# Loading and turning the first batch's queries in two parts, with moved loads, in a talking-heads attention and feed-forward kernel

## The chip, the cores and the metric

The kernel runs on one core of a Trainium2 chip. The metric is the device time of one execution in microseconds (us). The core has a matrix engine (TensorE, PE in the profile; its weight loads are PEld), VectorE (DVE), ScalarE (ACT), GpSimd (POOL) and SyncE (SP), which run their own instruction streams and wait for one another by semaphores, and sixteen DMA engines, which take work from queues. POOL issues the loads that change the type (float32 in memory, bf16 on the chip), SP the copies inside the core.

## The reference

For eight batches of twelve heads, 448 positions and 64 dimensions, with `w_pre` and `w_post` 12 by 12:

```python
scores = scale * np.matmul(q, k.transpose(0, 1, 3, 2))
scores = np.einsum('bhij,hg->bgij', scores, w_pre)
attn = softmax(scores)                       # over the last axis
attn = np.einsum('bhij,hg->bgij', attn, w_post)
x = np.matmul(attn, v)                       # heads side by side: 3584 x 768
h = np.maximum(x @ w_in, 0.0)                # w_in 768 x 2048
out = h * h @ w_out                          # w_out 2048 x 768
```

## The kernel before

**Steps.** A batch has 45 steps (`NT`) of ten queries each (`IQ`), so there are 360 steps, and one loop over `i` (line 578) writes out the order of TensorE and POOL by hand for all of them (`tc.manual_schedule`, line 524). The other engines' orders follow the program order and `tc.issue_after`. In step `i`, `mix` (line 456) makes the mixed scores of ten queries for all twelve heads at once, 120 rows, and ScalarE takes the exponential (line 471): the n-th exponential in the trace marks step n. POOL then scales `post` by the reciprocal sums (`pn`, line 481), and four steps later (`LAG`) `unmix` (line 487) multiplies the exponentials by it on TensorE; VectorE copies the result out of PSUM (line 502). After fifteen steps `av_unit` multiplies by the values, and when a batch is done `ffn1_unit` and `ffn2_unit` run as filler between the steps. PSUM has eight banks for all of this.

**Two ways to the mixed scores.** From step 20 on (`FUSED`), a *score burst* (line 394) multiplies 128 queries by all keys for a few heads at a time, ScalarE and VectorE copy the scores to a tile `S` (lines 416 and 418; two buffers), and SP's DMAs gather ten queries with all heads into a tile `G` (line 435; twelve buffers), on which line 467 does the mixing. A burst writes into a buffer that earlier gathers must have finished reading. `BURSTS` says at which gathers the bursts of the next block are made. In the first twenty steps there is no time for that: `mix_queries` (line 218) multiplies the turned queries by the mixing weights on VectorE, and `fused_part` (line 445) multiplies the keys by them, six matmuls per step.

**The front.** Queries and keys of the first batch come in twelve loads from POOL's queue (line 103), each of two heads on one half of the partitions: for `u` = 0, 1, 2 two of queries, then two of keys. Each row holds seven positions, since a partition holds seven consecutive positions (`RQ`), and `turn_unit` (line 227) transposes a unit of queries or keys with 28 small matmuls (line 239) and copies it out (line 241). While loads are on their way TensorE multiplies a zeroed tile (`still`, line 93). `mix_queries(u, 0, NEAR)` makes steps 0 to 3, `NEAR` to `SOON` steps 4 to 11, and `SOON` to `FUSED` steps 12 to 19. `make_identity` writes the matrix for the transposes with two POOL instructions.

**Later loads.** `KQ_AT`, `KQ_LATER`, `V1_AT`, `V_LATER`, `W1_AT`, `W2_AT` give the steps at which POOL issues the loads of queries and keys, values and weights of the next batches; the staging tiles of queries and of keys have one buffer each. `TURN` says at which step of a batch the next batch's keys (first three numbers) and queries are turned; the turn needs both halves of the load. The squares of the feed-forward's first half (line 320) are made by POOL, or by VectorE for columns from 300 on; `EARLY` starts those of the first batch by thirds of the columns, at steps 21, 29, 38 and 52.

Of the kernel before, what the change touches and what calls it, by code (L numbers as in the profile page):

```python
# [14 lines left out]
B, H, S, D = 8, 12, 448, 64  # L15
DMODEL = H * D
DFF = 2048
NPAIR = H // 2
FT = DFF // 128
R = 4  # L20
RQ = 7
PQ = S // RQ
HQ = H // 2
IQ = 10
# [2 lines left out]
FUSED = 20  # L27
SOON = 12
FQ = FUSED * IQ
NEAR = 4  # L30
# [2 lines left out]
BURSTS = {0: ([4, 8], [5, 8])}  # L33
for _b in range(1, B):
    STARTS[_b], FIRST[_b], BURSTS[_b] = (0, 128, 256, 384), (0, 13, 26, 39), ([5, 8], [5, 8], [6], [2, 4])
BURSTS[1] = ([5, 8], [7, 10], [6], [2, 4])
BURSTS[2] = ([7, 10], [5, 8], [6], [2, 4])
GATHERS_AT = 8
FIRST_AT = (3, 5, 7)
HALF = H // 2  # L40
TT = 15
TQ = TT * IQ
LAG = 4
AHEAD = 10
SCALE = 1.0 / 8.0
TURN = {0: (20, 22, 23, 24, 26, 27), 1: (24, 24, 24, 28, 28, 28), B: (2 + LAG,) * 3 + (17 + LAG,) * 3}
KQ_LATER = {1: (26, 28, 37, 41), B: (22, 25, 28, 31)}
V_LATER = {1: (30, 32, 34), B: (34, 37, 40)}
KQ_AT = {1: (4, 7, 10, 12), 2: (49, 51, 53, 55)}
W1_AT = (-1, 1, 3, 14, 16, 18)  # L50
W2_AT = (27, 29, 31, 33, 36, 39, 42, 45)
V1_AT = (46, 48, 24)
EARLY = ((21, 0, 0, 2), (29, 0, 2, 4), (38, 1, 0, 4), (52, 2, 0, 4))
FFN2_AT = 60
STILL = (10, 2, 2, 2, 1)
SOONEST = 3
MAIN = 3 * 128

# [2 lines left out]
def kernel(  # L61
# [36 lines left out]
    def stage_tile(name):  # L98
        return stage.tile([P, HQ, RQ, D], BF16, name=name, tag=name, bufs=1)

    def load(t, src, b, a, h0=0, h1=HQ):

        nc.gpsimd.dma_start(out=t[PQ * a:PQ * a + PQ, h0:h1, :, :].rearrange("p h r d -> p h (r d)"),
                            in_=src[b, HQ * a + h0:HQ * a + h1, :, :].rearrange("h (p r) d -> p h (r d)", r=RQ))

    staged = {}
    staged[0] = (stage_tile("qst"), stage_tile("kst"))
    ident = consts.tile([P, P], BF16, name="ident")
    for u in range(NPAIR // 2):
        for w, src in enumerate((q, k)):  # L110
            for x in range(2):
                load(staged[0][w], src, 0, x, 2 * u, 2 * u + 2)
                if u + w == 0 and x == 1:
                    masks.make_identity(nc, ident[:, :])

    def wcol(w, name, eng):
        t = consts.tile([P, H], F32, name=name)
# [106 lines left out]
                                    in1=wrep[:, u + 3 * y, :, :].unsqueeze(1).to_broadcast([P, t1 - t0, H, IQ]),  # L224
                                    op=ALU.mult)

    def turn_unit(b, which, u, eng=None):

        store, name = (qTs, "qT") if which == 0 else (kTs, "kT")
        if b not in store:  # L230
            store[b] = work.tile([P, NPAIR, S], BF16, name=name, tag=name, bufs=2)
        src = staged[b][which]
        got = [bank("tr_ps", BF16) for _ in range(2)]
        for r in range(RQ):
            c = PQ * (r if which == 0 or r == RQ - 1 else 2 * (r % 3) + r // 3)
            for hh in range(2):
                for x in range(2):
                    rs = slice(PQ * x, PQ * x + PQ)
                    nc.tensor.transpose(got[x][64 * hh:64 * hh + 64, c:c + PQ], src[rs, 2 * u + hh, r, :], ident[rs, rs])  # L239
        for x in range(2):  # L240
            (eng or nc.vector.tensor_copy)(out=store[b][:, u + 3 * x, :], in_=got[x][:, 0:S])

    def turn_units(b):
        return [(250, lambda u=u, w=w: turn_unit(b, w, u)) for w in (1, 0) for u in range(NPAIR // 2)]
# [56 lines left out]
    def ffn1_unit(b, ft, k=1, n0=0, n1=S):  # L301

        ps = bank("h_ps")
        n = n1 - n0
        for j in range(k):
            f = ft + j
            for c2 in range(NPAIR):
                nc.tensor.matmul(ps[:, n * j:n * j + n], lhsT=w1[f // 8][:, c2, f % 8 * 128:f % 8 * 128 + 128],  # L308
                                 rhs=xts[b][:, c2, n0:n1], start=(c2 == 0), stop=(c2 == NPAIR - 1))
        if n0 == 0 and ft % 2 == 0:  # L310
            h2ts[(b, ft // 2)] = ffnp.tile([P, 2, MAIN], BF16, name="h2", tag="h2", bufs=FT // 2 + 1)
        h2 = h2ts[(b, ft // 2)][:, ft % 2:ft % 2 + k, :]
        hr = ffnp.tile([P, S], F32, name="hr", tag="hr", bufs=2)
        nc.scalar.activation(out=hr[:, 0:k * n], in_=ps[:, 0:k * n], func=ACT.Relu)  # L314
        hr = hr[:, 0:k * n].rearrange("p (k n) -> p k n", k=k)
        eng = nc.vector if n0 >= 2 * TQ else nc.gpsimd
        last = tails[:, ft:ft + k, 64 * (b % 2):64 * (b % 2) + 64]
        for x, y, o, dst in ((n0, min(n1, MAIN), 0, h2), (max(n0, MAIN), n1, MAIN, last)):
            if x < y:
                eng.tensor_tensor(out=dst[:, :, x - o:y - o], in0=hr[:, :, x - n0:y - n0], in1=hr[:, :, x - n0:y - n0],  # L320
                                  op=ALU.mult)
# [202 lines left out]
    with tc.manual_schedule(engines={PE, POOL}):  # L524
# [1 line left out]
            load_v(0, x)  # L526
        still(STILL[0])
        for u in range(NPAIR // 2):
            turn_unit(0, 0, u)
            mix_queries(u, 0, NEAR)  # L530
            if u == 1:
                with tc.issue_after(mixes[(1, 0)].ins):
                    mix_queries(0, NEAR, SOON)
            if u == 2:
                for t in range(SOONEST):
                    fused_part(t, 0)
            else:
                still(STILL[1 + 2 * u])
            turn_unit(0, 1, u, nc.scalar.copy)
            if u < 2:  # L540
                still(STILL[2 + 2 * u])
        for t in range(SOONEST):
            fused_part(t, 1)
        with tc.issue_after(mixes[(2, 0)].ins):
            mix_queries(1, NEAR, SOON)
            mix_queries(2, NEAR, SOON)
        loads = {}
        ahead = [FUSED]

# [28 lines left out]
        for i in range(-1, end):  # L578
            for f in loads.get(i, []):
                f()  # L580
            if i < 0:
                continue
            if i == NT // 2:
                for (_, n), (t, order) in orders.items():
                    half_pre(n, t, order)
            s0 = steps[i] if i < len(steps) else None
            s1 = steps[i - LAG] if LAG <= i < len(steps) + LAG else None
            if s0:
                b, t = s0
                if t == 0:  # L590
                    if b + 1 < B:
                        for x, u in enumerate(turn_units(b + 1)):
                            at_step(i + TURN.get(b, TURN[B])[x], u)
            early = [x for x in bounds if x > i]
            rest = early[0] - i if early else (1 + LAG - i) % NT + 1
            rest = min(rest, end - i) if i > len(steps) - NT // 2 else rest
            share = sum(w for w, _ in filler) / rest / 2
            now = timed.pop(i, [])
            if s0:
                mix(s0)  # L600
            now_at[0] = i
            send_stores(i)
            for w, f in now:
                f()
                owed[0] -= w if not FFN2_AT <= i < 2 * NT else 0
            fill(share)
            if s1:
                unmix(s1)
                b1, t1 = s1
                if t1 % TT == TT - 1:  # L610
                    for u in av_units(b1, t1 // TT):
                        at_step(i + 3, u)
                if t1 == NT - 1:
                    at_step(i + 3 if b1 else FFN2_AT, (0, lambda b1=b1: filler.extend(ffn_units(b1))))
            if 2 < i < 6:
                with tc.issue_after(mixes[(2, NEAR)].ins):
                    mix_queries(i - 3, SOON, FUSED)
            if i in FIRST_AT:
                x = 2 * FIRST_AT.index(i)
                score_burst(0, 0, [x, x + 1])  # L620
            if i == 3:
                with tc.issue_after(mixes[(2, NEAR)].ins):
                    make_post()
                    make_orders()
                    clear_values()
            for _ in range(2 if i >= GATHERS_AT else 0):
                if ahead[0] > min(max(i + AHEAD, FIRST[0][1] - 1), len(steps) - 1):
                    break
                b2, t2 = steps[ahead[0]]
                gather((b2, t2))  # L630
                ahead[0] += 1
                blk2 = max(x for x in range(len(FIRST[b2])) if FIRST[b2][x] <= t2)
                nxt = blocks.index((b2, blk2)) + 1
                first = BURSTS[b2][blk2]
                if nxt < len(blocks) and t2 - FIRST[b2][blk2] in first:
                    x = first.index(t2 - FIRST[b2][blk2])
                    score_burst(*blocks[nxt], [3 * x, 3 * x + 1, 3 * x + 2])
                    if filler and filler[0][1] in second:
                        w, f = filler.pop(0)
                        f()  # L640
                        owed[0] -= w
            if i + 1 < end:
                fill(share)
# [35 lines left out]
```

## Time and profile before

| | |
|---|---|
| time, median of three runs | 583.04 us (582.56 to 585.91) |
| the profiled execution's own time | 583.95 us |
| its span, first to last instruction | 582.2 us |
| TensorE busy | 567.5 us (97%) |
| VectorE, ScalarE, POOL busy | 398.8, 379.7, 378.9 us |
| moved by DMA | 72.28 MB, mean 124 GB/s |
| chain that ended last | PE 89%, DMA 6%, ACT 2% |

The span is cut into stretches in the views below; the third column pair of a stretch is what each engine was busy. A chain of waits is followed back from the last instruction to whatever released each step. A name such as `L239` is a line of the kernel. The granted TensorE clock is 1.00 over the whole span.

### The profile page before, as it was taken

The numbers are of one execution on the slowest core, as the hardware profiler recorded it, in microseconds if no ns is written. First come the engines' busy times: TensorE is split into PE (matmuls) and PEld (weight loads), VectorE is DVE, ScalarE is ACT, GpSimd is POOL, SyncE is SP. The second block draws the span as 40 slices with busy tenths as digits, with TensorE's granted clock in tenths as the row PEclk, the third lists the DMA queues.
The fourth block names the chain that finished last, engine by engine and source line by source line (L and its number), as shares of the span: only waits on it lengthen the run. The fifth ranks groups of instructions, "written<-read, shape, count | busy, mean of one in ns | idle before, by whom it ended". The sixth has DMA issues, their size and how long they took to land.

```text
span 582.2 us, 18463 instructions
## 1 busy us (share of the span) xinstructions
PE 567.5 (97%) x6750; PEld 362.6 (62%) x6752; DVE 398.8 (69%) x980; ACT 379.7 (65%) x1090; POOL 378.9 (65%) x844
## 2 busy tenths in 40 slices
PE   7999999999999999999999999999999999999996
PEld 3667777556566566566566665666665665666554
DVE  6858868778676777866877668867877668655011
ACT  2768978588876557864877648775777548862410
POOL 6657985655877448774778547785577647774830
PEclk9999999999999999999999999999999999999999
DMA  9999998797568864796558954697544865422113
GB/s 130 159 193 184 187 199 173 152 168 175 111 108 149 145 128 87 126 157 141 101 100 135 176 117 93 120 145 154 107 73 71 137 139 104 84 46 55 29 27 82
DMA packets 84043, 72.28 MB, mean 124 GB/s; under 512 B 18768, under 2 KB 80496, under 8 KB 83952
## 3 DMA queue, kind: packets, MB, share of 16 engines
q0 software_dynamic: 37856, 33.04, 37.1%
q1 hardware_dynamic: 45514, 37.86, 29.5%
q8 instruction: 53, 0.87, 0.6%
q10 hardware_dynamic: 582, 0.21, 0.2%
q14 instruction: 38, 0.31, 0.1%
HBM read 47.28 MB, written 11.01 MB: 100 GB/s over the span
## 4 chain that ended last, share of the span: by engine, by line
PE 89%; DMA 6%; ACT 2%; POOL 1%; issue 1%; DVE 1%; ACTq 0%; POOLq 0%
PE h_ps L308 24%; PE o_ps L353 24%; PE m_ps L467 11%; PE at_ps L496 10%; PE ot_ps L254 5%; DMA G<-S 5%; PE s_ps L406 5%; PE m_ps L453 4%; PE tr_ps L239 2%; PE ot_ps L261 2%; PE at_ps L500 2%; DMA kst<-in_k_dram 1%; PE s_ps L412 1%; ACT e L471 1%; ACT S L416 1%
## 5 line engine op out<-in xcount | busy, mean ns | idle before, releaser
L502 DVE CAST at<-at_ps 128x480 bf16<-128x480 f32 (+1 forms) x360 | 206.6, 592 | 63.1 <-PE at_ps L500 46.0
L471 ACT ACTIVATE e<-m_ps 120x448 bf16<-120x448 f32 x360 | 195.7, 550 | 82.1 <-PE m_ps L467 45.4
L481 POOL TENSOR_SCALAR pn<-post,rc 120x120 bf16<-120x120 bf16 (+1 forms) x340 | 122.4, 370 | 137.6 <-DVE rc L478 76.0
L308 PE MATMUL h_ps<-xt,w 128*128 128x448 bf16 (+2 forms) x960 | 165.8, 315 | 1.0 <-ACT S L416 0.9
L353 PE MATMUL o_ps<-w,h 128*128 128x384 bf16 x768 | 138.8, 326 | 0.1
L467 PE MATMUL m_ps<-G,pre 120*120 120x448 bf16 (+1 forms) x340 | 121.3, 357 | 2.5 <-ACT S L416 1.4
L308 PEld LDWEIGHTS <-w 128*128 128x128 bf16 x960 | 83.4, 98 | 54.1 <-issue 4.9
L496 PE MATMUL at_ps<-pn,e 120*128 120x120 bf16 x1080 | 115.8, 215 | 1.3 <-POOL pn L481 1.1
L496 PEld LDWEIGHTS <-e 120*128 120x128 bf16 x1080 | 85.9, 98 | 45.7 <-issue 3.6
L320 POOL TENSOR_TENSOR h<-hr 128x384 bf16<-128x384 f32 (+1 forms) x128 | 103.1, 806 | 11.1 <-ACT hr L314 9.5
L353 PEld LDWEIGHTS <-h 128*128 128x128 bf16 x768 | 72.4, 98 | 50.5 <-issue 8.0
L314 ACT ACTIVATE hr<-h_ps 128x448 f32<-128x448 f32 (+2 forms) x136 | 72.0, 530 | 47.0 <-PE h_ps L308 39.4
L416 ACT CAST S<-s_ps 128x448 bf16<-128x448 f32 x177 | 82.3, 551 | 11.1 <-PE s_ps L406 7.2
L418 DVE CAST S<-s_ps 128x448 bf16<-128x448 f32 x141 | 80.0, 615 | 3.9 <-DMA G<-S 2.8
L471 ACT ACTIVATION_READ_ACCUMULATOR e<-m_ps 120x1 f32 x360 | 75.5, 210 | 0.0
L362 DVE COPY osb<-o_ps 128x384 f32<-128x384 f32 x54 | 30.0, 556 | 55.4 <-PE o_ps L353 55.3
L478 DVE RECIPROCAL rc<-sm 120x1 f32<-120x1 f32 (+1 forms) x192 | 31.0, 162 | 40.6 <-ACT e L471 28.0
L467 PEld LDWEIGHTS <-pre 120*120 120x120 bf16 (+1 forms) x340 | 45.0, 132 | 17.5 <-issue 8.6
L267 ACT CAST xt<-ot_ps 128x450 bf16<-128x450 f32 (+1 forms) x48 | 25.7, 534 | 26.7 <-PE ot_ps L261 26.3
L484 POOL TENSOR_TENSOR en<-e,rc 120x128 bf16<-120x128 bf16 (+1 forms) x112 | 42.8, 382 | 0.0
L254 PE MATMUL ot_ps<-at,v 128*64 128x150 bf16 x864 | 41.7, 229 | 0.0
L406 PE MATMUL s_ps<-kT,qT 64*128 64x448 bf16 x276 | 39.0, 352 | 0.2
(66 smaller groups left out, 502.7 us busy)
## 6 DMA issues: line engine op xcount, KB each, us to landing
G<-S SPq DMA_DIRECT2D x276, 105.0 KB
out_dram<-osb POOLq DMA_DIRECT2D x48, 192.0 KB, 4.7
kst<-in_k_dram POOLq DMA_DIRECT2D x14, 336.0 KB, 5.9
qst<-in_q_dram POOLq DMA_DIRECT2D x14, 336.0 KB, 5.8
G<-S SPq DMA_DIRECT2D x70, 52.5 KB
v<-in_v_dram POOLq DMA_DIRECT2D x8, 384.0 KB, 9.1
w<-in_moe_w_in_dram POOLq DMA_DIRECT2D x6, 512.0 KB, 8.5
w<-in_moe_w_out_dram POOLq DMA_DIRECT2D x8, 384.0 KB, 9.2
```

The lines of the kernel that those rows point to most:

```text
L254: nc.tensor.matmul(ps[64 * hh:64 * hh + 64, TQ * y:TQ * y + TQ], lhsT=vts[b % 2][:, g, r, :], rhs=at[:, r, g, :, :].rearrange("p t i -> p ...
L308: nc.tensor.matmul(ps[:, n * j:n * j + n], lhsT=w1[f // 8][:, c2, f % 8 * 128:f % 8 * 128 + 128], rhs=xts[b][:, c2, n0:n1], start=(c2 == 0 ...
L314: nc.scalar.activation(out=hr[:, 0:k * n], in_=ps[:, 0:k * n], func=ACT.Relu)
L320: eng.tensor_tensor(out=dst[:, :, x - o:y - o], in0=hr[:, :, x - n0:y - n0], in1=hr[:, :, x - n0:y - n0], op=ALU.mult)
L353: nc.tensor.matmul(ps[:, 0:384], lhsT=lhsT, rhs=w2[ft // 4][:, ft % 4, nt * 384:(nt + 1) * 384], start=(ft == 0), stop=(ft == FT - 1))
L416: nc.scalar.copy(out=sb[:, h, :], in_=ps[:, 0:S])
L418: nc.vector.tensor_copy(out=sb[:, h, :], in_=ps[:, 0:S])
L467: nc.tensor.matmul(ps[0:n, 0:S], lhsT=m[0:n, 0:n], rhs=Gs.pop(s)[0:n, :], start=True, stop=True)
L471: nc.scalar.activation(out=e[0:n, x, :], in_=ps[0:n, 0:S], func=ACT.Exp, scale=SCALE, accum_out=sm[0:n, x:x + 1])
L481: nc.gpsimd.tensor_scalar(out=esb[(b, t - z)][1][0:rows, :], in0=(post_gi if fused else post)[0:rows, :], scalar1=rc[0:rows, z:z + 1], sca ...
L496: nc.tensor.matmul(ps[:, RG * r:RG * r + RG], lhsT=e[0:n, tl % 2, P * r:P * r + P], rhs=pn[0:n, :], start=True, stop=True)
L502: nc.vector.tensor_copy(out=ats[(b, third)][:, 0:k, :, tl, :], in_=ps[:, 0:k * RG].rearrange("p (r g i) -> p r g i", r=k, i=IQ))
```

## The change

The first batch's queries are loaded in two parts: first positions 0 and 1 of each row (`RF = 2`, 128 of the 448 columns) for all heads, two loads in place of six; then the keys; then the other five positions, two loads. The identity is cleared by VectorE, and POOL's other instruction for it stands among the key loads. The first part of the queries is turned and mixed ahead of all keys; the second part is turned in step 3 of the loop. The mixing of steps 4 to 11 is done in two blocks of four steps. One of the six copies of turned keys goes from ScalarE to VectorE. The zeroed tile is multiplied 19 times in place of 17. Score bursts and gathers of the first batch move by one step. Loads of batches one to three, two turns and one pair of bursts get other steps. Four squares of 300 columns (third 1, `ft` 8 to 14) go from POOL to VectorE.

```diff
+RF = 2
-BURSTS[1] = ([5, 8], [7, 10], [6], [2, 4])
+BURSTS[1] = ([5, 8], [7, 10], [6], [3, 5])
-GATHERS_AT = 8
-FIRST_AT = (3, 5, 7)
+GATHERS_AT = 9
+FIRST_AT = (4, 6, 8)
+REST_AT = 3
-TURN = {0: (20, 22, 23, 24, 26, 27), 1: (24, 24, 24, 28, 28, 28), B: (2 + LAG,) * 3 + (17 + LAG,) * 3}
-KQ_LATER = {1: (26, 28, 37, 41), B: (22, 25, 28, 31)}
-V_LATER = {1: (30, 32, 34), B: (34, 37, 40)}
-KQ_AT = {1: (4, 7, 10, 12), 2: (49, 51, 53, 55)}
+TURN = {0: (20, 22, 23, 24, 26, 27), 1: (20, 20, 20, 28, 28, 28), B: (2 + LAG,) * 3 + (17 + LAG,) * 3}
+KQ_LATER = {1: (22, 24, 37, 41), B: (22, 25, 28, 31)}
+V_LATER = {1: (53, 55, 57), B: (34, 37, 40)}
+KQ_AT = {1: (4, 7, 10, 12), 2: (52, 54, 58, 61)}
-V1_AT = (46, 48, 24)
+V1_AT = (46, 49, 24)
-STILL = (10, 2, 2, 2, 1)
+STILL = (13, 3, 3)
...
-    def load(t, src, b, a, h0=0, h1=HQ):
+    def load(t, src, b, a, h0=0, h1=HQ, r0=0, r1=RQ):
...
+    for x in range(2):
+        load(staged[0][0], q, 0, x, r1=RF)
+    nc.vector.memset(ident[:, :], 0.0)
     for u in range(NPAIR // 2):
-        for w, src in enumerate((q, k)):
-            for x in range(2):
-                load(staged[0][w], src, 0, x, 2 * u, 2 * u + 2)
-                if u + w == 0 and x == 1:
-                    masks.make_identity(nc, ident[:, :])
+        for x in range(2):
+            load(staged[0][1], k, 0, x, 2 * u, 2 * u + 2)
+        if u == 1:
+            masks.make_identity(nc, ident[:, :], nomemset=True)
+    for x in range(2):
+        load(staged[0][0], q, 0, x, r0=RF)
...
-    def turn_unit(b, which, u, eng=None):
+    def turn_unit(b, which, u, engs=None, r0=0, r1=RQ):
...
-        for r in range(RQ):
+        for r in range(r0, r1):
...
-            (eng or nc.vector.tensor_copy)(out=store[b][:, u + 3 * x, :], in_=got[x][:, 0:S])
+            copy = engs[x] if engs else nc.vector.tensor_copy
+            copy(out=store[b][:, u + 3 * x, PQ * r0:PQ * r1], in_=got[x][:, PQ * r0:PQ * r1])
...
-        eng = nc.vector if n0 >= 2 * TQ else nc.gpsimd
+        eng = nc.vector if n0 >= 2 * TQ or n0 and ft >= FT // 2 else nc.gpsimd
...
         for u in range(NPAIR // 2):
-            turn_unit(0, 0, u)
+            turn_unit(0, 0, u, r1=RF)
             mix_queries(u, 0, NEAR)
-            if u == 1:
-                with tc.issue_after(mixes[(1, 0)].ins):
-                    mix_queries(0, NEAR, SOON)
+        still(STILL[1])
+        for u in range(NPAIR // 2):
             if u == 2:
+                with tc.issue_after(mixes[(2, 0)].ins):
+                    mix_queries(0, NEAR, 2 * NEAR)
+
+            def between(out, in_):
+                with tc.issue_after(mixes[(0, NEAR)].ins):
+                    mixes["kT"] = nc.vector.tensor_copy(out=out, in_=in_)
+
+            turn_unit(0, 1, u, (nc.scalar.copy, nc.scalar.copy if u < 2 else between))
+            if u == 0:
+                still(STILL[2])
+            else:
                 for t in range(SOONEST):
-                    fused_part(t, 0)
-            else:
-                still(STILL[1 + 2 * u])
-            turn_unit(0, 1, u, nc.scalar.copy)
-            if u < 2:
-                still(STILL[2 + 2 * u])
-        for t in range(SOONEST):
-            fused_part(t, 1)
-        with tc.issue_after(mixes[(2, 0)].ins):
-            mix_queries(1, NEAR, SOON)
-            mix_queries(2, NEAR, SOON)
+                    fused_part(t, u - 1)
+        for t0 in range(NEAR, SOON, NEAR):
+            with tc.issue_after(mixes["kT" if t0 == NEAR else (2, t0 - NEAR)].ins):
+                for u in range(t0 == NEAR, NPAIR // 2):
+                    mix_queries(u, t0, t0 + NEAR)
...
-            if 2 < i < 6:
-                with tc.issue_after(mixes[(2, NEAR)].ins):
-                    mix_queries(i - 3, SOON, FUSED)
+            if i == REST_AT:
+                for u in range(NPAIR // 2):
+                    turn_unit(0, 0, u, r0=RF)
+            if FIRST_AT[0] <= i < FIRST_AT[0] + 3:
+                with tc.issue_after(mixes[(2, SOON - NEAR)].ins):
+                    mix_queries(i - FIRST_AT[0], SOON, FUSED)
...
-                with tc.issue_after(mixes[(2, NEAR)].ins):
+                with tc.issue_after(mixes[(2, SOON - NEAR)].ins):
                     make_post()
```

## The prediction

> **What bounds the kernel now.** I read the page's first part, then TensorE by stretches, the timeline of TensorE and POOL at the front, the chain, and the waits of the two stretches with holes.
>
> ```profile
> PE 567.5 (97%) x6750; PEld 362.6 (62%) x6752; DVE 398.8 (69%) x980; ACT 379.7 (65%) x1090; POOL 378.9 (65%) x844
> ```
>
> TensorE is the bound: of a span of 582.2 us it is idle 14.7. Any saving must come out of those, or out of work on TensorE that no one needs (the zeroed tile). The table of stretches (length, then busy us of PE, PEld, DVE, ACT, POOL) shows where they are:
>
> ```profile
> 0.00:14.74 14.74, 10.64 (x190) 4.98 (x193) 9.04 (x32) 3.21 (x5) 10.13 (x21) 1.00 0.92 131
> 14.74:30.00 15.26, 15.20 (x102) 9.52 (x103) 12.61 (x34) 10.70 (x31) 9.98 (x20) 1.00 1.09 156
> 75.00:90.00 15.00, 12.72 (x200) 10.37 (x198) 9.73 (x24) 10.94 (x34) 14.29 (x29) 1.00 1.18 199
> 105.00:120.00 15.00, 13.04 (x251) 7.99 (x250) 11.90 (x33) 8.38 (x28) 9.09 (x21) 1.00 0.89 163
> 577.72:582.20 4.48, 0.00 (x1) 0.00 (x0) 0.36 (x1) 0.32 (x1) 0.00 (x0) 1.00 0.20 56
> ```
>
> The tail (4.48) is not touched. Idle is 2.28 at 75 to 90 and 1.96 at 105 to 120; 180 to 530 has 0.6 in all. The first 14.74 us look 10.64 busy, but the work in them that counts is 168 transposes at 0.34 us per 28 (2.04) and six matmuls at 0.19 (1.14): 3.2 us. The rest is zeroed tile and waiting for loads. TensorE's timeline shows the last key unit, the chain shows what comes behind it:
>
> ```profile
> 13.50 0.21 PE L239 MATMUL tr_ps<-ident,kst 64*64 64x64 bf16 x1
> 14.33 0.41 PE L239 MATMUL tr_ps<-ident,kst 64*64 64x64 bf16 x27 [0.61 <-DMA kst<-in_k_dram]
> ```
>
> ```profile
> 8.41 5.87 DMA kst<-in_k_dram
> 14.29 0.04 issue
> 14.33 0.41 PE tr_ps L239 x27
> 14.74 3.54 PE m_ps L453 x18
> ```
>
> The twelfth load, issued at 8.41, lands at 14.29; from there TensorE has no hole. So the front is worth what the last key load comes earlier. Its issue waits in POOL's queue:
>
> ```profile
> 2.68 0.22 POOL masks.py:197 MEMSET ident<- 128x128 bf16 x1
> 2.83 0.59 POOL L103 DMA_DIRECT2D kst<-in_k_dram  x1
> ...
> 4.34 1.19 POOL L103 DMA_DIRECT2D qst<-in_q_dram  x2
> 5.51 1.22 POOL L103 DMA_DIRECT2D kst<-in_k_dram  x2
> 6.67 1.24 POOL L103 DMA_DIRECT2D qst<-in_q_dram  x2
> 7.83 1.25 POOL L103 DMA_DIRECT2D kst<-in_k_dram  x2
> ```
>
> Two issues take 1.17 us from start to start, 0.58 each.
>
> **Part 1, keys earlier.** Four query loads (4 x 0.58 = 2.33) and the clearing of the identity (2.83 - 2.68 = 0.15) leave the queue ahead of the last key load; the other identity instruction stays ahead. It is issued at 8.41 - 2.48 = 5.93. The twelve loads take 4.1, 4.6 (median) and 5.9 us to land. With the median it lands at 10.5, with its own 5.87 at 11.8. The other bound is the DMA engines: by the trace's packet records a load now is 128 packets of 896 bytes at 88 ns, 11.3 engine-us, and one such load lands every 0.575 us, so 19.6 engine-us are done per us. The new first query loads are 2 x 384 packets of 256 bytes, which the trace lacks; 128 bytes take 32 ns and 384 take 51, so about 41.5: 32 engine-us. Up to the last key this is 32 + 6 x 11.3 = 100 in place of 135: 1.8 us less, 12.5. A cause of the late landing may go: from 12.11 an instruction fetch of 16 KB holds one DMA engine for 0.95 us. Range 10.6 to 12.5; TensorE itself can't be there before about 10.9 (first queries near 6.9, then turns, zeroed tile and six matmuls). I take 11.4, the middle: **-2.9** (-1.8 to -3.4).
>
> *A rule against this part.* The Trainium skill (DMA: Bandwidth & Descriptors, Specifications) gives 512 bytes as the least transfer for line rate, with read-modify-write below. The trace shows no step there: 384 bytes take 51 ns, 512 take 60. It can't show 256.
>
> **Part 2, queries turned later.** The 60 transposes of step 3 used to run under load waits and now stand in a full stream: 60 x 0.34 / 28 = **+0.73**. Their loads: issued near 6.5 and 7.2, 2 x 384 packets of 640 bytes at about 69.5 ns (between 512 at 60 and 896 at 88) are 53 engine-us, 2.7 us behind the last key: 13.9, or 15.2 with the late bound. Step 3 comes at 11.4 + 0.4 + 3.5 = 15.3, so I cost the wait at 0; were its cover gone, 1 us. Values and first weights queue behind these loads; POOL's order only brings them forward.
>
> **Part 3, VectorE at the front.** Steps 4 to 11 cost 12 x 0.400 in place of 6 x 0.653: +0.88. The key copy adds 0.39; it waits for the last key turn, and mixes for steps 4 to 11 of `u` 1 and 2 queue behind it, first needed in step 4, four us later. Second query copies, six of 320 columns at 0.386 x 320 / 448, add 1.65 behind 14 us that used to be done by 13. Together 2.9 us; 14.74 to 30 had 2.65 idle. TensorE feels it when copies free PSUM banks late; later steps have slack (9.5 of 15 busy at 30 to 45). Between 0 and 2.9, nearer the low end since the banks buffer two or three steps: **+0.3**.
>
> **Part 4, squares.** Four of 0.68 us (starts 77.7, 80.2, 82.6, 85.0) leave POOL, which is 14.29 of 15 busy there. The longest hole names POOL:
>
> ```profile
> PE at_ps L496 <- POOL pn L481: 1.1, 1, 1.1
> ```
>
> But `pn` began at 78.38 and its reciprocal ended at 78.19, so the square ahead cost 0.2; the lateness came from a weight load's issue, a value load's issue and a square that stays. VectorE has room (9.73 of 15); on 168 columns it took 0.33 to 0.50, so some 0.6 for 300. Gain 0 to 1.1, **-0.3**, near the row.
>
> The skill (SBUF — State Buffer, the passages on the shared port pair) says that a VectorE instruction with two SBUF inputs excludes GpSimd reads for its length. The trace agrees in part: a VectorE square of 128 columns took 0.77 beside POOL's at 85.0, 0.28 alone. Then the last term would be nearer 0.
>
> **Part 5, bursts and loads of 100 to 120.** The waits there:
>
> ```profile
> ACT S L416 <- DMA G<-S: 2.6, 1, 2.6
> DVE S L418 <- DMA G<-S: 2.4, 1, 2.4
> PE m_ps L467 <- ACT S L416: 1.4, 1, 1.4
> ```
>
> The burst at the third gather of batch 1's last block writes a buffer whose last gather lands at 116.7. One gather later is one step, about 1.3 us; two key loads (109.5, 112.4) move four steps ahead and value loads (114.7 to 121.3) 23 steps back, so the gather itself should land sooner (7.1 now; 5 with less traffic is an estimate). Both together exceed 2.6. Bounds 0.5 to 1.8, **-1.5**.
>
> **Part 6, the rest.** Turning batch 2's keys moves from step 69 to 65, with loads at steps 52 and 54 in place of 49 and 51. The fourth bursts' shift and gathers from step 9 lie far ahead of step 20. Zeroed tile: two more, at 0.43 us, in the wait for the first queries. All 0 in the forecast; the turn is a rival.
>
> **Sum.** -2.9 + 0.73 + 0.3 - 0.3 - 1.5 = -3.7. The profiled execution, 583.95, becomes 580.3; it was 0.91 above the median, so the median goes from 583.04 to **579.4**. With all terms at their better ends it is -5.6 (-3.4 + 0.73 - 1.1 - 1.8), at their worse ones, VectorE's apart, -1.6 (-1.8 + 0.73 - 0.5).
>
> **Rivals.**
> - *The small packets drain slowly* (14%): 256 bytes at twice my price, 83 ns, put 32 engine-us, 1.6 us, ahead of the keys: -2.1, 580.9. Against: 128 bytes take 32 ns. This is what the skill's rule would do here.
> - *VectorE binds the fused steps* (12%): all 2.9 us reach TensorE in place of 0.3: -1.1, 581.9. For it: 12.61 of 15.26 busy before. Against: TensorE idles 0.06 there now.
> - *Slower: the key turn at step 65 waits* (11%). Batch 2's key loads took 13.5 to 15.0 us to land, at 80 to 103, since weight and value loads stand ahead in the queue. The second is now issued at step 54, about 86.7 in today's times; 15.0 later is 101.7. Step 65 begins at 98.5, 2.2 earlier if the front's gain reaches it while the saturated queue doesn't move: 5.4 us of waiting, all on TensorE, whose order is fixed. -3.7 + 5.4 = +1.7: 584.7. It decides from 3.7 us on. Against: the queue is first come first served, and today's load, with the same bytes ahead, lands at 97.3.
> - *More holes close* (13%): the front at its best (-3.4), the holes of 1.09 at 77.7 and 0.87 at 87.7, 0.3 at 82.5, and all 1.96 of 105 to 120: -3.4 + 0.7 - 4.2 = -6.9, 576.2.
>
> **Chances.** The forecast has 50%, its own range 577.4 to 581.5 (these two ends). Range with the rivals: 576.2 to 584.0, leaving out most of the slower rival and what lies beyond the better one. Under 1%, 5.8 us, a measurement of this kernel hardly tells from no change: faster needs less than 577.2, the better rival and a little of the forecast, 15%; slower needs over 588.9, a share of the turn's rival, 5%; within, 80%.
>
> **What would show it.** The last key turn at 10.9 to 12.5 and the 18 matmuls right behind it; 60 transposes just before step 4, without a hole; VectorE's copies at most a step behind in 12 to 28; no wait of ScalarE's or VectorE's `S` copies for gathers near 110 to 115; no wait for a key load at step 65. Wrong if new holes appear in 12 to 30 or near 96, or if holes at 120 to 180 (0.98 now) grow as gains are given back there.

## The result and the profile after

The changed kernel takes 579.5 us (median of seven runs, 578.05 to 581.1) against 583.04 before: ratio 0.9936, 95% interval 0.9912 to 0.9961. The forecast was 579.4. The profiled execution is the slowest of the seven, 581.1 us with a span of 579.2.

TensorE's own line, and its stretches (length, then busy us of PE, PEld, DVE, ACT, POOL, clock, DMA share, GB/s), of the changed kernel:

```profile
PE 567.4 (98%) x6753; PEld 363.4 (63%) x6754; DVE 403.3 (70%) x998; ACT 379.5 (66%) x1089; POOL 377.1 (65%) x837
```

```profile
0.00:14.74 14.74, 12.60 (x147) 6.20 (x149) 8.96 (x39) 4.75 (x10) 9.37 (x18) 1.00 0.97 124
...
14.74:30.00 15.26, 15.11 (x160) 9.38 (x158) 14.83 (x44) 9.82 (x31) 11.89 (x23) 1.00 1.20 180
...
75.00:90.00 15.00, 12.91 (x186) 10.76 (x185) 9.46 (x24) 9.88 (x29) 8.70 (x20) 0.89 1.13 190
...
105.00:120.00 15.00, 14.66 (x197) 9.37 (x195) 12.34 (x32) 10.94 (x35) 8.75 (x23) 1.00 0.75 165
```

TensorE is busy for as long as before; its idle time fell from 14.7 to 11.8 us. The front is fuller, the stretch from 105 to 120 has lost its hole (0.34 idle), VectorE has hardly any room left from 14.74 to 30, and 75 to 90 is as full of holes as before (2.09), now with a lower clock. The front, first TensorE's timeline, then POOL's:

```profile
9.36 1.35 PE L460 MATMUL m_ps<-kT,w 128*120 128x448 bf16 x6
10.64 0.21 PE L245 MATMUL tr_ps<-ident,kst 64*64 64x64 bf16 x1
11.63 0.41 PE L245 MATMUL tr_ps<-ident,kst 64*64 64x64 bf16 x27 [0.79 <-DMA kst<-in_k_dram]
11.97 3.62 PE L460 MATMUL m_ps<-kT,w 128*120 128x448 bf16 x18
15.52 0.73 PE L245 MATMUL tr_ps<-ident,qst 64*64 64x64 bf16 x60
```

```profile
2.80 2.64 POOL L105 DMA_DIRECT2D kst<-in_k_dram  x4
5.51 0.32 POOL masks.py:199 TENSOR_SCALAR_AFFINE_SELECT ident<-ident 128x128 bf16<-128x128 bf16 x1
5.75 1.22 POOL L105 DMA_DIRECT2D kst<-in_k_dram  x2
6.93 1.37 POOL L105 DMA_DIRECT2D qst<-in_q_dram  x2
```

The last keys are turned from 11.63 in place of 14.33, with the 18 matmuls and the 60 transposes behind them and no hole between. Of this lead 1.8 us are left at step 45 (71.8 against 73.6). At step 55 nothing is left (86.4 against 86.3). The chain of waits and two-microsecond stretches show where it went:

```profile
64.16 14.66 DMA G<-S
78.82 0.04 issue
78.87 0.63 PE m_ps L474
```

```profile
76.00:78.00 2.00, 0.78 (x7) 0.30 (x4) 1.89 (x5) 1.30 (x5) 1.96 (x5) 1.00 1.11 248
78.00:80.00 2.00, 1.13 (x13) 0.75 (x15) 0.06 (x1) 0.47 (x2) 1.07 (x4) 0.62 1.25 183
80.00:82.00 2.00, 2.00 (x50) 2.00 (x46) 0.17 (x1) 0.70 (x3) 1.41 (x4) 0.53 1.44 188
```

A gather that the chain follows for 14.66 us lets TensorE stand still for 1.94 us, from 76.93 to 78.87, and the clock is at half from 78.47 to 81.88 (the clock column of the last two lines), so the first 3.0 us of work behind the hole run at half speed, which costs about 1.5 us more. After that the kernel wins the time once more: 2.9 us ahead at step 85, 3.2 at step 100. So the total came out as forecast in this execution although a piece of it was lost on the way; whether that piece belongs to the change is what most of the experiments ask.

### The profile page after: what moved, and what is told of

The parts are those of the page before. It is cut to its first block, busy times and chain, and to the rows that moved or that the text cites. A ratio compares the mean times of both kernels' runs of the same rounds, so it can differ in the third digit from the quotient of the medians.

```text
span 579.2 us, 18480 instructions
## 1 busy us (share of the span) xinstructions
PE 567.4 (98%) x6753; PEld 363.4 (63%) x6754; DVE 403.3 (70%) x998; ACT 379.5 (66%) x1089; POOL 377.1 (65%) x837
## 4 chain that ended last, share of the span: by engine, by line
PE 89%; DMA 4%; POOL 1%; DVE 1%; ACT 1%; issue 1%; SPq 1%; ACTq 0%; POOLq 0%
PE o_ps L360 25%; PE h_ps L315 24%; PE m_ps L474 11%; PE at_ps L503 10%; PE ot_ps L261 6%; PE s_ps L413 5%; DMA G<-S 3%; PE tr_ps L245 2%; PE m_ps L460 2%; PE ot_ps L268 2%; PE at_ps L507 2%; PE s_ps L419 1%; DMA kst<-in_k_dram 1%; ACT e L478 1%; SPq L445 1%
## 5 line engine op out<-in xcount | busy, mean ns | idle before, releaser
L478 ACT ACTIVATE e<-m_ps 120x448 bf16<-120x448 f32 x360 | 195.6, 550 | 85.2 <-PE m_ps L474 51.1
L327 POOL TENSOR_TENSOR h<-hr 128x384 bf16<-128x384 f32 (+1 forms) x124 | 100.3, 809 | 11.6 <-ACT hr L321 10.2
L507 PE MATMUL at_ps<-post,en 120*128 120x120 bf16 x181 | 39.1, 216 | 0.0
```

The costliest lines, as they stand in the source:

```text
L478: nc.scalar.activation(out=e[0:n, x, :], in_=ps[0:n, 0:S], func=ACT.Exp, scale=SCALE, accum_out=sm[0:n, x:x + 1])
```

## The experiments

The theory: the terms add up, the front about 1.9 us and bursts with loads about 1.5. The rival: the DMA engines bind from 50 to 90, so the front's lead is handed back there and all of the gain comes from the rest. The yardstick beside the times is the idle time of TensorE by stretch, in us, and the time at which step 20 begins, each read from one execution's trace. The three later rows without a ratio (before and front alone again, three positions first) are single executions; for the ratios before was timed anew beside each group of kernels:

| kernel | ratio to before, 95% interval | step 20 | idle 70:92 | idle 105:125 | idle 125:180 |
|---|---|---|---|---|---|
| before | | 43.8 | 2.37 | 2.04 | 0.91 |
| before, again | | 43.1 | 1.74 | 0.50 | 0.00 |
| changed | 0.9936 (0.9912 to 0.9961) | 42.0 | 2.34 | 0.34 | 0.70 |
| changed, again | 0.9940 (0.9917 to 0.9963) | 42.0 | 3.46 | 0.08 | 1.01 |
| front alone | 0.9962 (0.9933 to 0.9991) | 40.9 | 2.10 | 0.17 | 1.18 |
| front alone, again | | 41.6 | 1.51 | 0.18 | 1.65 |
| all but the front | 0.9960 (0.9926 to 0.9993) | 43.9 | 1.29 | 0.84 | 1.35 |
| bursts back | 0.9969 (0.9940 to 0.9998) | 41.5 | 2.95 | 1.23 | 0.77 |
| loads back | 0.9967 (0.9938 to 0.9995) | 41.2 | 2.18 | 1.87 | 0.99 |
| squares back | 0.9939 (0.9916 to 0.9962) | 41.6 | 1.10 | 0.47 | 0.09 |
| three positions first | | 43.1 | 1.95 | 0.40 | 0.60 |
| weights spread | 0.9918 (0.9895 to 0.9942) | 41.3 | 0.80 | 1.44 | 0.18 |
| keys later | 0.9904 (0.9868 to 0.9939) | 41.6 | 0.21 | 0.15 | 1.00 |
| all moved | 0.9912 (0.9878 to 0.9947) | 41.6 | 2.37 | 0.15 | 0.05 |

**The front alone.** From the changed kernel, back to the values before (the diffs of this part are written short, several tables to a line):

```diff
-BURSTS[1] = ([5, 8], [7, 10], [6], [3, 5])
+BURSTS[1] = ([5, 8], [7, 10], [6], [2, 4])
-    1: (20, 20, 20, 28, 28, 28)        # in TURN
+    1: (24, 24, 24, 28, 28, 28)
-KQ_LATER 1: (22, 24, 37, 41)  V_LATER 1: (53, 55, 57)  KQ_AT 2: (52, 54, 58, 61)  V1_AT (46, 49, 24)
+KQ_LATER 1: (26, 28, 37, 41)  V_LATER 1: (30, 32, 34)  KQ_AT 2: (49, 51, 53, 55)  V1_AT (46, 48, 24)
-        eng = nc.vector if n0 >= 2 * TQ or n0 and ft >= FT // 2 else nc.gpsimd
+        eng = nc.vector if n0 >= 2 * TQ else nc.gpsimd
```

> The front of the change alone (two-part query load, its turns and mixes, zeroed tile, first bursts and gathers a step later), with the bursts of batch 1, the later loads and turns and the squares as before. Additive theory (the terms of the prediction add up): last key turn near 11.6, step 45 about 1.8 us earlier than before, and the end 1.8 to 2.2 us earlier than before. Rival (the DMA engines bind between 57 and 90, so a lead of TensorE is handed back as late gathers there): the same 1.8 us at step 45, but 0 to 0.5 us at the end, with a longer hole on a gather between 75 and 90.

580.78 us against 583.15, 2.4 us. By the times the lead reaches the end; the rival's 0 to 0.5 us lies at the interval's edge (0.9991 is 0.5 us). Single executions don't show it: this one is at step 45 at 70.7 us, the two of before at 73.6 and 72.9; at step 120 it is at 170.3, those at 174.9 and 170.9. Unexpected: the stretch from 105 to 125 has no hole, with bursts and loads as before.

```profile
105.00:125.00 20.00, 19.83 (x285) 12.98 (x283) 16.30 (x43) 14.34 (x46) 14.79 (x34) 1.00 1.03 175
```

**All but the front.** The same lines set the other way in the kernel before.

> Everything but the front (bursts of batch 1, later loads and turns, four squares on VectorE). Additive theory: 1.5 to 2 us earlier than before, out of the holes at 105 to 120. Rival (the front's lead is handed back, so the whole gain is here): 3 to 3.5 us earlier.

580.79 us, 2.4 us as well, between the two expectations. The two parts alone give 2.4 + 2.4 = 4.8, both together 3.5 to 3.6; each has an uncertainty of 1.7 to 2.0 us, so they may add up or overlap by 1 us, and these runs don't tell which.

**Bursts back, loads back.** Only the first pair of lines above, or only the load and turn steps:

> The changed kernel with the bursts of batch 1's last block back at the second and fourth gather. If the burst's place closed the hole at 116: a hole of about 1.4 us is back at 112 to 117, and the time is 1 to 1.5 us over the changed kernel. Rival (the loads that left that stretch closed it): no hole over 0.4 us there, and 0 to 0.3 us.

> The changed kernel with loads of batches one to three and the key turn of step 65 as before. If the burst's place alone closed the hole at 116: 0 to 0.5 us over the changed kernel. Rival (the loads closed it): the hole of 1 us or more is back at 112 to 117 and the time is 1 to 1.5 us over. If the new load steps cause the late gather at 77: that hole (1.94 us) shrinks below 1.1 us, and the time is up to 1 us under.

581.23 and 581.36 us: by the ratios (0.9969 and 0.9967 against 0.9936 and 0.9940) either costs the changed kernel 1.6 to 1.9 us, with intervals that overlap, and leaves no more than the front alone has. The changed kernel was not timed beside these kernels, so they are compared only through before. In both the `S` copies wait for gathers again; the waits near 105 to 125 of bursts back, then of loads back (us in total, times, longest):

```profile
ACT S L423 <- DMA G<-S: 2.2, 1, 2.2
DVE S L425 <- DMA G<-S: 2.0, 1, 2.0
...
PE m_ps L474 <- ACT S L423: 1.0, 1, 1.0
```

```profile
DVE S L425 <- DMA G<-S: 2.0, 1, 2.0
ACT S L423 <- DMA G<-S: 1.8, 1, 1.8
PE m_ps L474 <- ACT S L423: 1.8, 1, 1.8
```

In the changed kernel these two waits are 0.3 and 0.6. So in these two executions one move without the other doesn't close the hole. It doesn't follow that both are needed: the front alone has neither move and no hole there (0.17 idle). The third expectation for loads back came half true: no hole near 77 is over 0.66 us, but they sum to 2.18 as before, and the time is over the changed kernel's and not under it.

**The two kernels once more.**

> The changed kernel once more, to see which of its holes stay. If the hole on a gather near 77 (1.94 us, with 3.4 us of half clock behind it) belongs to the change: holes of 1.5 us or more in all between 70 and 92, as in the other runs with the new front (2.0 to 2.8), and a lead over before that is smaller at step 55 than at step 45. Rival (chance of one execution): less than 1 us there and the full lead of 1.8 to 2.9 us at step 55. Time 579 to 580.5 us.

> The kernel before once more: are its holes at 75 to 90 (2.28 us) and 105 to 120 (1.96) the same in another execution? If they belong to the schedule, each is within 1 us of that.

> The front alone once more. Its first execution had no hole at 116 though bursts and loads stood as before. If the hole depends on how far the earlier holes put TensorE behind the gathers (chance): here 0.5 to 2 us at 105 to 120. If the front removes it: below 0.3 us again.

The changed kernel gave 579.35 us, with the holes between 70 and 92 again (3.46 us, the longest 1.72, but no half clock), and step 55 at 86.3 against 86.3 and 85.2 in the two executions of before. So they came twice; that they belong to the change isn't shown, for before idles 2.37 and 1.74 us in that stretch itself, and squares back, below, has the same loads and 1.10. The kernel before repeated one of its own holes (1.60 idle from 75 to 90, against 2.28) and not the other. Its second execution took 579.96 us, with this in place of the 17.96 busy of the first:

```profile
105.00:125.00 20.00, 19.50 (x323) 12.85 (x309) 15.77 (x43) 14.13 (x45) 13.81 (x32) 1.00 0.98 168
```

So the hole at 116, on which the fifth part of the prediction rests, is in one of two executions. The second is an unusual one: it is faster than all 70 timed runs of before (580.25 to 588.41), so how often the hole comes isn't known. The front alone had 0.18 there once more, and 1.65 in 125 to 180: with the new front and the old steps the waiting sits later. Why the front moves it is open. It also had a hole of 1.38 us at 66, which the table's stretches leave out, and stood at step 45 only at 72.8.

**Squares back.**

```diff
-        eng = nc.vector if n0 >= 2 * TQ or n0 and ft >= FT // 2 else nc.gpsimd
+        eng = nc.vector if n0 >= 2 * TQ else nc.gpsimd
```

> The changed kernel with the four squares on POOL again. If they are worth what the prediction gave them: 0.3 us over the changed kernel, with POOL over 11 us busy of the 15 from 75 to 90. Rival (POOL's lateness made the hole at 77.7): a hole of about 1 us on pn at 74 to 78 and 1 us over.

578.71 us, the changed kernel's ratio to within 0.0001. TensorE waits for `pn` 0.6 us once, and all its idle time from 70 to 92 is 1.10:

```profile
70.00:92.00 22.00, 20.90 (x307) 17.33 (x306) 16.27 (x44) 19.17 (x59) 16.68 (x35) 1.00 1.05 193
```

The move of the squares is worth nothing that can be measured; the interval of 1.3 us to either side would hide 0.3. That the long gather waits near 77 are missing here, with the loads of the changed kernel, is not explained by the squares' time, and may be chance.

**Three positions first.**

```diff
-RF = 2
+RF = 3
```

> The changed kernel with three positions of each row in the first query loads in place of two (192 columns, packets of 384 bytes). If the last key lands by the DMA engines' pace: 2 x 384 packets of 51 ns in place of 41 are 7.7 engine-us more, so it lands 0.4 us later than in runs of the changed front (10.2 to 11.6), and step 3 has 48 transposes, 0.58 us, in place of 60. Rival (the last key lands by POOL's issue): no later, within 0.1 us of the issue's own shift.

In the one execution, of 580.26 us, the last key load, issued at 6.25, lands at 12.04; in the ten executions with two positions it is issued at 6.34 to 6.37 and lands at 10.2 to 11.6, 10.92 on average. Later, which the rival doesn't have; but by 1.1 us and not 0.4, and the very first load already landed 1.3 us later than on average (6.91 in place of 5.4 to 6.2). So the lateness is there before any key is loaded, and one execution doesn't tell whether the wider packets or a late start made it. The last turn, at 12.56, stood behind six matmuls (11.28 to 12.63) and no longer waited for the load. The 48 transposes of step 3 take 0.60 us.

**Weights spread.** To take load off the DMA engines before 75:

```diff
-W2_AT = (27, 29, 31, 33, 36, 39, 42, 45)
+W2_AT = (27, 30, 33, 36, 39, 42, 45, 48)
-KQ_AT 2: (52, 54, 58, 61)    V1_AT = (46, 49, 24)
+KQ_AT 2: (50, 52, 59, 62)    V1_AT = (54, 56, 24)
```

> The changed kernel with the eight loads of the second weight three steps apart (27 to 48 in place of 27 to 45), batch 2's keys at 50 and 52, batch 1's values at 54 and 56, batch 2's queries at 59 and 62. If the DMA engines bind between 50 and 80 and make gathers late there: loads land in 8 us or less in place of 8 to 10, the holes between 70 and 92 fall below 1 us, no half clock, and the time is 1.5 to 3 us under the changed kernel. Rival (the holes come from ScalarE and POOL, which are busy there): holes of 1.5 us or more stay, and the time is within 0.7 us.

577.98 us, 1.4 under the changed kernel timed beside it, a little short of the 1.5 to 3 expected. The long hole on a gather is gone; one of 0.66 us at 75.7 is left:

```profile
70.00:92.00 22.00, 21.20 (x312) 17.65 (x310) 18.47 (x52) 19.77 (x61) 14.95 (x32) 1.00 1.10 198
```

TensorE is busy 21.20 us there against 19.66 (of which a part at half clock) and 18.54. The first five of these loads land in 7.8 to 8.5 us, in the changed kernel in 7.1 to 9.5, and the seventh in 7.8 against 10.3. ScalarE and POOL aren't less busy (19.77 and 14.95, against 16.41 and 13.19), so the rival falls. Over all the executions of the table, with these loads (weights spread, keys later) TensorE idles 0.80 and 0.21 us there, with the changed kernel's (changed twice, bursts back, squares back, three positions first) 1.10 to 3.46. This fits loads beside the gathers as what makes them late, and doesn't show it: each kernel was traced once or twice, squares back lies near weights spread, and in keys later the same loads take 7.7 to 9.5 us, as long as in the changed kernel, without a hole. Two waits took the place of the hole, 1.3 us for `S` copies at 112.6 and 0.6 for values at 97.

**Keys later, all moved.** Aimed at those two waits. The first on top of weights spread; the second has the other steps in place of that kernel's:

```diff
-KQ_LATER 1: (22, 24, 37, 41)
+KQ_LATER 1: (32, 34, 37, 41)
...
+W2_AT = (27, 30, 33, 36, 39, 41, 44, 46)    KQ_AT 2: (48, 50, 59, 62)    V1_AT = (53, 55, 24)
```

> The kernel of weights_spread with batch 3's keys loaded at steps 77 and 79 in place of 67 and 69. If loads beside the gathers hold back the bursts' copies: the hole of 1.28 us at 112.6 falls below 0.4 us and the time is about 1 us under weights_spread (577 us). Rival (the gathers are late by their own number): the hole stays, within 0.5 us.

> As keys_later, with the second weight's loads at 27, 30, 33, 36, 39, 41, 44, 46, batch 2's keys at 48 and 50 and batch 1's values at 53 and 55, so that the values land before step 67 (in weights_spread a hole of 0.63 us at 97 waits for them). No hole on values, and 0.5 us under keys_later if the denser weights cost nothing between 70 and 92; else holes over 1 us there and no gain.

578.08 and 578.04 us, so neither gains on weights spread (577 was expected of keys later). With the keys later the `S` copies wait no more (0.15 idle from 105 to 125), and TensorE's longest wait is for the values:

```profile
PE ot_ps L261 <- DMA v<-in_v_dram: 1.6, 1, 1.6
```

All moved closes that (0.23 idle at 92 to 105) and opens 2.37 at 70 to 92, with the denser weights. All three lie 1.3 to 1.5 us under the changed kernel's medians; among them, and against it, the intervals overlap.

## Why the prediction was right

**Part 1, keys earlier: right, with too short an issue and too slow a drain.** Forecast -2.9. In three executions with the old front the last key turn begins at 14.33, 13.44 and 14.19, mean 13.99; in ten with the new one at 10.49 to 11.63, mean 11.05: -2.9. The last load is issued at 6.36, not 5.93: the two query loads, of three times the packets, held POOL's queue for 1.53 us (1.41 before), and the fourth key load follows the third by 0.86 in place of 0.58, for a reason that no run shows. It then lands at 10.2 to 11.6, on average 4.56 us after its issue, like the median load of before (4.6); the DMA bound, 12.5, was too late, and taking the middle of the two was luck in part. Nor does the floor of 10.9 from TensorE's own work hold: the first queries landed at 5.4 to 6.2, not 6.9, and four of the ten turns begin before 10.9. In two executions (front again, loads back) the load lands 0.5 us before TensorE is through with its six matmuls, so there it isn't the limit any more. Packets of 256 bytes take 41 ns and of 640 bytes 69 (forecast 41.5 and 69.5), so the rival of the slow small packets is out. So is the read-modify-write below 512 bytes of the Trainium skill (DMA: Bandwidth & Descriptors, Specifications) as a cost that shows here: 128, 256, 384 and 512 bytes take 32, 41, 51 and 60 ns, on one line. The instruction fetch of 16 KB comes at 12.4 to 14.3 with the new front, behind the last keys.

**Part 2, queries later: right.** The 60 transposes take 0.73 us; their loads landed at 13.1 and 14.35, the turn stood at 15.52, and nothing waited.

**Part 3, VectorE: right.** It is busy 14.83 of 15.26 us from 14.74 to 30 (12.61 before), and TensorE idles 0.15 there in place of 0.06, so the term is nearer 0.1 than 0.3. The front in all is what step 20 shows: 43.6 on average with the old front, 41.5 with the new, 2.1 us. The terms gave -2.9 + 0.73 + 0.3 = -1.9. Alone it is worth 2.4 us at the end.

**Part 4, squares: not seen,** and 0.3 is below what these times can tell. They take 0.46 to 0.54 us on VectorE (forecast 0.6). POOL's time was indeed no cause: 8.70 busy of 15 from 75 to 90 now, and holes as before, on gathers.

**Part 5, bursts and loads: the size fits, the evidence was weaker than it looked.** Forecast -1.5; taking either half out costs 1.6 to 1.9, and everything but the front alone gives 2.4, with intervals that hold 1.5. That both halves are needed, as the prediction had it, agrees with the ratios, whose intervals overlap, and not with the front alone, where the hole is closed without either. The waits were read from one execution, and the next one of the same kernel had a quarter of the idle time there. So the size came out, and why the moves gain it stays open; that it came out is luck in part.

**Part 6, the key turn: right.** It is the only turn of a later batch that the change moves. The second key load of batch 2, issued at 86.11, landed at 95.57; the turn began at 98.23 and had no wait for it. With the later issues the loads land in 7.9 to 11.1 us (three of the four; the fourth's landing is not in the trace) in place of 13.5 to 15.0; with the new front and the old steps (front alone) they take 13.2 to 14.0. The slower rival is out.

**What it missed:** the gather holes at 74 to 79, 1.94 us and half a clock in one execution, 3.46 us in all from 70 to 92 in the other. The prediction asked whether the front's lead would be given back at 120 to 180; in these executions it was given back at 77. It looked at the late gathers as a wait of bursts, not as a limit on how far TensorE may run ahead. That the sum still held is due to the rest: between steps 70 and 100 the changed kernel won 3.4 us against the profiled execution of before, which had the hole at 116. Against the second execution of before it won none: step 100 begins at 142.5 and 142.0 in the two of the changed kernel and at 142.4 there. So the times show a gain of 3.5 us, and the traces show 2.1 us of it at the front; where the rest comes from is open.

## What to carry to other kernels

When loads at the front are the wait, count what stands ahead of the last one that is needed, both in the issuing queue and in bytes, and move behind it whatever the first steps don't use; the matmuls that then run in the full stream are the price. A lead at the front may be given back where the transfers further on don't follow (here 1.8 us at step 45 and none at step 55), so look at the loads of the next hundred microseconds again; the three kernels that spaced them here came out 1.3 to 1.5 us lower, within their intervals. A hole of one execution is no property of the schedule until a second execution shows it.

## What the runs showed of the hardware

A hole on TensorE can cost twice. In the changed kernel's first execution the granted clock was 0.5 for 3.4 us, from 1.54 us into a hole of 1.94 (two short holes of 0.17 and 0.15 stood before it). Six matmuls with the values took 0.57 us in it and 0.36 right behind. In loads back it was 0.5 for 3.4 us too, from 0.7 us behind the end of a hole of 1.76. The stretches of that kernel:

```profile
114.00:116.00 2.00, 0.34 (x5) 0.26 (x4) 0.07 (x1) 0.49 (x2) 1.96 (x6) 1.00 1.20 201
116.00:118.00 2.00, 1.82 (x7) 0.90 (x7) 1.65 (x3) 2.00 (x7) 1.04 (x2) 0.71 1.31 192
118.00:120.00 2.00, 2.00 (x12) 0.93 (x11) 0.73 (x2) 0.49 (x3) 1.07 (x3) 0.50 1.42 210
```

Holes of 1.72, 1.64 and 1.42 us in other executions had no such step behind them. The Trainium skill (TensorE: Matmul & The Clock Gate, Part 1: The HAM clock gate) puts the step down after an idle window of about 3.4 us. The 3.4 us of half clock agree with its window; the holes of 1.94 and 1.76 us are shorter.

One kernel's executions differ by as much as the change is worth: the two of before have spans of 582.2 and 578.2 us, with 14.7 and 10.6 us of idle TensorE, the difference lying in the front (4.10 and 2.61 to 14.74) and in the waits behind it (5.4 and 2.5 from 70 to 180).
